# Threshold attention and ELU FFN on one core: the first sequence walked by query blocks instead of by pairs

## Chip, core and metric

The kernel runs on one core of a Trainium2 chip. The metric is the device time of one execution, in microseconds. Before the change it is 1313.69 us (median of 4 runs, 1313.1 to 1314.35).

## What is computed

Eight sequences (batch B = 8) of 576 tokens, 8 heads of 64 columns, all in fp32. Each query keeps only the keys whose score lies within tau of its best score; the attention output, 4608 tokens of 512 columns, goes through a feed-forward network (FFN) with an ELU between two matrices.

```python
scores = (q @ k.T) / 8
thresh = max(scores, axis=-1) - tau
scores = where(scores >= thresh, scores, -1e9)
attn = exp(scores - max(scores)); attn = attn / (sum(attn) + 1e-9)
x = (attn @ v)            # heads side by side: (4608, 512)
h = x @ w_in              # (4608, 2048)
g = where(h > 0, h, exp(min(h, 0)) - 1)
out = g @ w_out           # (4608, 512)
```

The weights come in as 64-bit floats, so they have to be turned into fp32 on the chip.

## The kernel before, in words

**Tiles.** Two heads make a pair; a sequence has NPAIR = 4 pairs, and there are 32 in all. The 576 queries of a pair are cut into four blocks of 128 for each head (i = 0 to 3, "two-head" steps) and the last 64 queries of both heads together (i = NC = 4, a "one-head" step): NB = 5 steps a pair. `steps` lists them as (pair, block).

**A step.** `scores` (L364) writes the scores of one block against all keys to PSUM, one tile for each head. `max_of` (L402, VectorE, here DVE) takes the negative maximum, `bound_of` (L406, GpSimd, here POOL) the threshold, `exp_of` (L416, ScalarE, here ACT) the exponential, `mask_of` (L425, DVE) multiplies it by the comparison with the threshold and sums the row. `reciprocal_of` (L431, L432) and `normalize` (L398, POOL) follow, in place in the tile w. Then w has to be transposed so that keys lie on partitions. There are two ways: `turn_parts` transposes 128x128 blocks on TensorE (PE, L435) into PSUM tiles rt and copies them on ACT (L451) to wTa or wTb; `turn_squares` (L509) transposes squares of 32x32 on DVE, writes them to DRAM ("there") and `fetch` reads them back in the right order. `values` (L570, L575) multiplies the transposed weights by v once a "part" is there: part 0 is blocks 0 and 1 (tile wTa), part 1 blocks 2, 3 and 4 (tile wTb, wider). `values_out` (L692, L698) copies the result to xt, the FFN's input.

**Fillers.** Where PE has little to do, `room` in `turn_parts` issues transposes of the identity into the same rt tile before the real ones, as many as were put in the list `spare`; `idle` does the same near the start.

**FFN.** The first sequence's 512 tokens (without the tails of 64) go through a plain FFN in two chunks of 256: `ffn1` (L733, with exp, minus one and ELU at L740, L743, L747) and `ffn2_plain` (L773). Each unit is cut in two halves; there are 64 halves. `needs` says how many of the 32 weight pieces must be converted before a unit may start. All later tokens use products with fewer multiplications (L1229, L1369), which need sums and differences of weight blocks: `make_in` (L852 to L854, DVE) writes three sums of each of eight units to DRAM ("win_sums"), `change_in` and `change_out` (POOL) change the weights in place.

**Weight pieces.** Each of the 32 pieces is loaded (`load_w`, 512 KB, tile wst, 4 buffers) and converted: `convert_rest` (L240, ACT), `convert_shift` (L246, DVE), `convert_add` (L252, POOL), `convert_abs` (L257, ACT), `convert_end` (L265, DVE).

**The order.** For the first 45 steps (MIDDLE = 45) `early_tasks` makes a list of tasks. Each has a due time: `begin` of its step plus an offset written in the code plus an offset from the table MOVED under a key such as "mask0b2" (task, head, stage letter, block). `do` runs tasks by due time, but any task that one needs runs first. The result is one fixed order of instructions for each engine and DMA queue; the due times themselves set no wait. The stages before the change:

- steps 0 to 19 (sequence 0, `per_seq` = 20): pair by pair; three score tiles in PSUM; fillers; no FFN;
- at step 20 `switch` closes the pool of three score tiles and opens two score tiles and two FFN banks;
- steps 20 to 34: the FFN halves by SHARES, two weight pieces a step;
- steps 35 to 44 (from SWITCH = 35): the tile pool "late" is there, every step is turned by `turn_squares`, the sums of `make_in` are made one unit a step, FFN halves by QUOTA (4, 4, 2, 3, 2).

SQUARES holds the steps turned on DVE: all from SWITCH on, and those of steps 22 to 34 whose MOVED entry "sq.." is over 1.0, which before the change is only step 33.

After step 44 another planner writes the wide part: scores of two blocks at a time (L622, L669 for the 64-query block), interleaved with the FFN of the sequence before. It runs from the first L669 at 289.8 us to the end.

Of the kernel before, what the change touches and what calls it, by code (L numbers as in the profile page):

```python
# [19 lines left out]
    "adda10": 2.75, "adda40": -0.7, "addb10": -0.45, "addb11": -0.96, "addb20": 0.4, "addb21": 0.54, "addb30": 0.08,  # L20
    "addb31": 0.42, "addb40": -0.13, "addb41": -0.45, "addz40": 1.52, "chd0": -1.67, "chd1": 0.66, "chd3": 5.2,
    "cka3": 1.4, "ckb3": -3.64, "ckc3": -0.46, "ckd3": -1.83, "ckz3": -1.37, "cqa2": 6.78, "cqb2": -3.01,
    "cqc2": -0.22, "cqd2": 2.27, "enda10": 2.38, "enda40": -0.2, "endb00": -0.03, "endb01": 1.48, "endb10": -0.28,
    "endb20": -1.25, "endb21": -1.07, "endb30": 1.25, "endb31": -0.02, "endb40": -0.99, "endb41": 0.29,
    "endz40": 1.58, "exp0a0": 0.24, "exp0a1": -1.03, "exp0a2": 0.05, "exp0a3": 1.07, "exp0a4": -0.35, "exp0b1": -0.97,
    "exp0b2": -0.37, "exp0b3": 1.51, "exp0b4": 0.45, "exp0c0": 0.41, "exp0c1": 3.53, "exp0c2": 0.65, "exp0c4": -0.53,
    "exp0d0": 0.12, "exp0d1": -2.91, "exp0d4": -0.42, "exp0z0": -1.78, "exp0z1": -0.69, "exp0z2": -1.71,
    "exp0z3": 1.1, "exp0z4": -1.32, "exp1a0": 0.27, "exp1a2": -1.45, "exp1b0": -0.12, "exp1b1": -0.6, "exp1b2": 0.26,
    "exp1b3": -0.56, "exp1c0": -1.22, "exp1c1": 1.42, "exp1c3": -0.54, "exp1d1": 0.28, "exp1d3": 0.23, "exp1z0": 4.71,
    "exp1z2": 0.39, "exp1z3": 2.23, "f0.0": -2.08, "f1.0": -0.13, "f1.1": 0.2, "f10.0": 0.05, "f11.0": -0.04,  # L30
    "f12.1": 0.12, "f13.1": -0.5, "f14.0": 0.02, "f15.1": -0.06, "f16.0": 0.04, "f16.1": 0.69, "f16.2": -0.14,
    "f17.0": -0.28, "f18.1": 0.12, "f2.0": -5.54, "f2.1": -0.25, "f2.2": 0.7, "f20.1": -1.03, "f21.0": 0.13,
    "f22.1": -0.19, "f23.0": 0.08, "f23.1": 2.72, "f23.2": 0.07, "f25.0": 0.39, "f26.0": -0.08, "f26.1": 0.42,
    "f3.0": 0.35, "f5.0": -0.32, "f5.1": 4.32, "f6.1": -0.54, "f7.0": -0.01, "f9.0": 0.35, "f9.1": 1.94,
    "fbound0": -0.14, "fbound1": 0.93, "fbound4": -0.36, "fe00": 0.1, "fe10": 0.37, "fe11": 0.3, "fe20": -0.6,
    "fetchc0": 0.68, "fetchc1": 1.8, "fetchc3": 1.11, "fetchc4": 2.68, "fetchd0": -1.89, "fetchd1": -3,
    "fetchd2": 0.42, "fexp00": 0.1, "fexp20": 0.25, "fexp31": 0.12, "ffetch0": 1.19, "ffetch1": -0.24,
    "ffetch2": -0.52, "ffetch3": -0.65, "fkcopy": -0.11, "floadk": -2.59, "floadq": 2.51, "fm00": -3.15,
    "fm01": -0.49, "fm11": -2.07, "fm20": 1.6, "fm21": -0.43, "fmask00": 1.48, "fmask01": -0.63, "fmask10": 0.68,
    "fmask11": 0.02, "fmask30": -0.16, "fmask31": 0.36, "fmask4": 0.2, "fmax00": -0.03, "fmax01": -0.65,  # L40
    "fmax10": 0.91, "fmax11": 0.5, "fmax20": -0.99, "fmax21": -0.15, "fmax30": 0.04, "fmax31": -0.17, "fmax4": 0.36,
    "fnorm01": 0.83, "fnorm10": -0.23, "fnorm11": -0.44, "fnorm20": 1.68, "fnorm31": -0.75, "fout1": 0.83,
    "fsum0": 0.21, "fsum2": 0.33, "fsum3": 0.21, "fturn0": 0.21, "fturn2": 0.46, "fturn3": -1.27, "fturn4": -3.36,
    "fx0": -0.43, "fx10": 3.03, "fx11": 2.86, "fx2": 1.4, "fx3": 0.53, "fx6": -1.72, "fx8": -0.33, "fx9": 1.95,
    "half0b0": 2.6, "half0b2": 0.03, "half0b4": -1.89, "half0c0": -0.35, "half0c1": 3.13, "half0c2": -1.05,
    "half0c3": 0.43, "half0c4": 0.59, "half0d0": 0.33, "half0d1": 2.22, "half0d2": 2.32, "half0d3": 1.9,
    "half0d4": -0.23, "half1b0": -0.69, "half1b2": 4.21, "half1b3": 2.24, "half1c0": -0.27, "half1c1": 1.44,
    "half1c3": -0.41, "half1d0": -1.15, "half1d1": -0.81, "half1d3": -1.93, "half2b0": 0.57, "half2b1": 3.37,
    "half2b2": 1.47, "half2b4": 4.56, "half3a4": -0.25, "half3b0": -0.69, "inc0": 0.26, "inc1": -0.32, "inc2": -0.84,
    "inc3": 0.62, "inc4": 1.01, "ind0": 3.59, "ind1": -0.55, "ind2": 0.71, "lka4": 0.31, "lkb4": -0.23, "lkc4": 2.75,  # L50
    "lkd4": -1.7, "lkz4": 1.33, "lqa3": -0.05, "lqb3": -0.78, "lqc3": 3.06, "lqd3": 1.57, "lqz3": 3.59, "lva3": -6.41,
    "lvb3": 0.23, "lvc3": -6.29, "lvd3": 0.25, "lwa40": -0.35, "lwb00": -0.29, "lwb01": 3.86, "lwb11": -1.49,
    "lwb20": 5.29, "lwb21": -0.43, "lwb30": 0.12, "lwb31": 0.49, "lwb41": -1.26, "lwz40": -0.42, "mask0a0": 1.44,
    "mask0a1": -0.72, "mask0a2": -1.16, "mask0a3": -0.52, "mask0a4": 0.63, "mask0b0": 2.64, "mask0b1": -0.06,
    "mask0b2": 4.79, "mask0b3": 0.64, "mask0b4": -0.11, "mask0c0": -1.59, "mask0c1": 3.33, "mask0c3": 0.31,
    "mask0c4": 0.37, "mask0d0": 3.54, "mask0d1": -0.89, "mask0d2": 0.28, "mask0d3": 1.22, "mask0z0": 1.27,
    "mask0z1": 2.9, "mask0z2": 0.32, "mask0z3": 1.31, "mask0z4": 0.56, "mask1a0": 1.27, "mask1a1": -0.16,
    "mask1a2": -4, "mask1a3": 1.13, "mask1b0": 3.3, "mask1b1": 1.74, "mask1b2": -0.32, "mask1b3": -0.38,
    "mask1c0": -1, "mask1c1": 2.6, "mask1c3": 0.06, "mask1d0": 3.74, "mask1d1": 0.12, "mask1d2": -0.2,
    "mask1d3": -0.98, "mask1z0": 0.69, "mask1z1": -1.47, "mask1z2": 0.5, "mask1z3": -4.11, "max0a0": -0.3,  # L60
    "max0a1": 1.72, "max0a2": 0.59, "max0a3": -0.46, "max0a4": 0.01, "max0b2": 1.44, "max0b3": 2.43, "max0b4": 0.13,
    "max0c0": 1.5, "max0c2": -3.36, "max0c3": -0.04, "max0c4": 1.16, "max0d0": 0.78, "max0d1": 2.46, "max0d2": -0.18,
    "max0d3": -0.86, "max0d4": 0.16, "max0z0": 2.5, "max0z1": -1.46, "max0z2": 6.32, "max0z3": -1.37, "max0z4": -0.85,
    "max1a0": 0.61, "max1a1": -0.07, "max1a2": -0.77, "max1a3": -0.22, "max1b0": 0.78, "max1b2": 0.03, "max1b3": 1.55,
    "max1c0": 0.62, "max1c1": -3.37, "max1c2": 1.27, "max1c3": -0.06, "max1d0": 0.68, "max1d1": -0.28, "max1d2": 3.35,
    "max1d3": 0.21, "max1z0": 2.29, "max1z1": 2.67, "max1z2": 9, "max1z3": 2.6, "norm0a0": 0.2, "norm0a1": -1.45,
    "norm0a2": -4.39, "norm0a3": -1.9, "norm0a4": -1.3, "norm0b1": -1.86, "norm0b4": -1.38, "norm0c0": 1.41,
    "norm0c1": -1.7, "norm0c3": 2.54, "norm0c4": 0.59, "norm0d0": 0.35, "norm0d1": 3.1, "norm0d2": -2.58,
    "norm0d3": -0.7, "norm0d4": -0.09, "norm0z0": -2.03, "norm0z1": -3.22, "norm0z2": -2.15, "norm0z3": -1.83,
    "norm0z4": -0.25, "norm1a0": -0.02, "norm1a1": -0.55, "norm1a2": 0.15, "norm1b0": 0.05, "norm1b1": 1.56,  # L70
    "norm1b2": -0.1, "norm1b3": -0.03, "norm1c0": -0.9, "norm1c1": 3.66, "norm1d0": -1.5, "norm1d1": -0.05,
    "norm1d2": -0.42, "norm1d3": -1.5, "norm1z0": 5.01, "norm1z1": -1.89, "norm1z2": -0.52, "norm1z3": -0.76,
    "outa4": -0.11, "outb1": -0.97, "outb4": -0.24, "outc1": 2.48, "outc4": -1.41, "outd1": -0.33, "outz1": 2.43,
    "outz4": -1.2, "part0a0": 0.88, "part0a1": 0.83, "part0a2": 0.68, "part0a3": -1.25, "part0b0": -0.58,
    "part0b1": -0.24, "part0b2": -0.82, "part0b3": -0.08, "part0b4": -1.67, "part0z2": -1.94, "part0z4": 0.79,
    "part1a1": -1.63, "part1a2": -1.63, "part1a3": -1.33, "part1a4": -2.94, "part1b0": 0.5, "part1b1": -1.16,
    "part1b2": 5.58, "part1b3": 1.91, "part1b4": -0.68, "part1z0": -4.29, "part1z1": -0.2, "part1z2": -0.4,
    "part1z3": 1.37, "part1z4": -1.08, "part2a0": -1.64, "part2a1": 3.26, "part2a2": 6.12, "part2a3": 1.34,
    "part2b0": 0.62, "part2b2": -0.41, "part2b3": 0.06, "part2z0": 2.23, "part2z1": 1.82, "part2z3": 0.07,
# [58 lines left out]
def kernel(  # L138
# [12 lines left out]
    P = 128  # L151
# [63 lines left out]
    for t in qds + vds:  # L215
        nc.gpsimd.memset(t, 0.0)
# [43 lines left out]
    def convert_end(i):  # L260

        progress[0] = i + 1
        if i in staged:
            sign, top = staged.pop(i)[:, :, 1].bitcast(I32), tops.pop(i).bitcast(FP32)
            nc.vector.scalar_tensor_tensor(pieces[i][1], top, 0.0, sign, ALU.max, ALU.mult)  # L265


    raws, pairs = {}, {}


    def load(pr, parts=("qm", "km", "v"), shared=False, queue=nc.sync):
# [649 lines left out]
    def early_tasks():  # L921
# [117 lines left out]
        for n in range(MIDDLE):  # L1039
# [8 lines left out]
            if n == per_seq:  # L1048
                task("switch", t, None, switch, *rooms)
# [591 lines left out]
```

## Time and profile before

The profiled execution took 1313.82 us and its span is 1312.0 us.

| what | before |
|---|---|
| PE busy (matmuls) | 1295.2 us, 99% |
| PEld busy (weight loads) | 1008.2 us, 77% |
| DVE busy | 1016.8 us, 77% |
| ACT busy | 559.5 us, 43% |
| POOL busy | 803.1 us, 61% |
| DMA, mean | 190 GB/s |
| first score, step 0 | 8.2 us |
| first score, step 10 | 53.4 us |
| first score, step 20 | 98.5 us |
| first score, step 35 | 208.2 us |
| first wide score (L669) | 289.8 us |

How to read it. A row "line engine op out<-in" names the line of the kernel, the engine and the tiles. PE is the matmul row and PEld the loads of its stationary operand, which overlap. In a table by windows, each engine's figure is its busy time in that stretch and (x..) its instructions. In a timeline, the first number is the start and the second the busy time of a group of like instructions; matmuls are pipelined, so the distance from one start to the next says what one costs the queue. An fp32 matmul of the program shows as two in the trace, a transpose as one. A bracket gives the idle time before the instruction and who ended it.

### The profile page before, as it was taken

To read this page: it belongs to the slowest core of one execution; us is meant where nothing else is said; L and a number is where in the kernel's file an instruction comes from. 1 tells how busy PE (TensorE), PEld (TensorE's weight loads), DVE (VectorE), ACT (ScalarE), POOL (GpSimd) and SP (SyncE) were. 2 spreads that over 40 slices of the span, in tenths; PEclk is the share of its full clock that TensorE was granted. 3 is DMA by queue.
4 is the path that set the end of the run, shared out by engine and by line. 5 is a ranking of instruction groups with operands and counts; after the bars stand their busy time and mean duration, and the time that the engine had idled before them with its cause. 6 is when DMAs were issued, how large, how long until landed. Compare 5 with 4: busy or idle time off the path is not lost.

```text
span 1312.0 us, 21958 instructions
## 1 busy us (share of the span) xinstructions
PE 1295.2 (99%) x6971; PEld 1008.2 (77%) x6971; DVE 1016.8 (77%) x2198; ACT 559.5 (43%) x1216; POOL 803.1 (61%) x1186
## 2 busy tenths in 40 slices
PE   9999999999999999999999999999999999999998
PEld 7667656546888787777778787777777888888887
DVE  5878886878888988898889979897989882545534
ACT  5767773225253535344444435352525260421320
POOL 4657874767567665766576747574858473624533
PEclk9999999999999999999999999999999999999999
DMA  6344655888888988898989888989899874221211
GB/s 137 77 103 123 165 126 140 239 231 214 231 232 237 266 224 250 216 264 212 245 216 257 236 226 234 252 239 240 233 253 252 219 220 171 92 73 61 92 61 32
DMA packets 323315, 248.94 MB, mean 190 GB/s; under 512 B 208768, under 2 KB 285056, under 8 KB 323200
## 3 DMA queue, kind: packets, MB, share of 16 engines
q1 hardware_dynamic: 320832, 247.25, 69.2%
q8 instruction: 55, 0.90, 0.3%
q10 hardware_dynamic: 2368, 0.30, 0.2%
q14 instruction: 60, 0.49, 0.1%
HBM read 162.40 MB, written 85.07 MB: 189 GB/s over the span
## 4 chain that ended last, share of the span: by engine, by line
PE 91%; DVE 4%; DMA 2%; POOL 1%; issue 1%; ACT 1%; SPq 1%; ACTq 0%; DVEq 0%; POOLq 0%
PE f L1369 29%; PE f L1229 28%; PE sc L622 8%; PE sc L682 7%; PE f L773 4%; PE rt L435 4%; PE sc L364 3%; PE f L733 3%; PE pv L575 2%; PE sc L674 1%; PE sc L669 1%; PE pv L570 1%; DVE w L425 1%; POOL w L398 0%; DMA vd<-in_v_dram 0%
## 5 line engine op out<-in xcount | busy, mean ns | idle before, releaser
L398 POOL TENSOR_SCALAR w<-w,rs 128x576 f32<-128x576 f32 x196 | 164.4, 846 | 81.8 <-DVE rs L432 64.7
L629 DVE TENSOR_REDUCE mx<-sc 128x1 f32<-128x576 f32 x207 | 148.3, 750 | 35.7 <-PE sc L622 33.0
L639 ACT ACTIVATE w<-sc,mx 128x576 f32<-128x576 f32 x115 | 83.0, 740 | 114.4 <-DVE mx L629 96.8
L1229 PE MATMUL f<-xt,sw 128*128 128x256 f32 x512 | 123.8, 384 | 0.9 <-ACT xt L692 0.5
L1229 PE MATMUL f<-xt,w_in_sb 128*128 128x256 f32 x512 | 122.4, 381 | 0.3 <-ACT w L1243 0.3
L635 POOL TENSOR_SCALAR th<-mx,ntau 128x2 f32<-128x2 f32 (+1 forms) x115 | 34.3, 298 | 141.7 <-DVE mx L629 141.7
L509 DVE STREAM_TRANSPOSE x<-w 128x512 f32<-128x512 f32 (+2 forms) x146 | 98.2, 706 | 13.3 <-POOL w L398 12.9
L1229 PEld LDWEIGHTS f<-xt,w_in_sb 128*128 128x128 f32 x512 | 96.1, 190 | 16.0 <-ACT w L1243 3.2
L1229 PEld LDWEIGHTS f<-xt,sw 128*128 128x128 f32 x512 | 93.7, 190 | 18.3 <-ACT xt L692 0.9
L622 PE MATMUL sc<-kT,qT 64*128 64x512 f32 (+4 forms) x736 | 107.5, 423 | 0.0
L1229 PE MATMUL f<-x,w_in_sb 128*128 128x256 f32 x448 | 106.1, 379 | 1.4 <-ACT g L1290 1.4
L1369 PE MATMUL f<-w_out_sb,g 128*128 128x256 f32 x448 | 107.1, 382 | 0.0
L622 PEld LDWEIGHTS sc<-kT,qT 64*128 64x128 f32 x736 | 80.8, 186 | 34.3 <-issue 16.8
L1369 PE MATMUL f<-w_out_sb,s 128*128 128x256 f32 x448 | 107.0, 382 | 0.0
L1369 PE MATMUL f<-t,s 128*128 128x256 f32 x448 | 105.8, 379 | 0.0
L1316 POOL TENSOR_TENSOR s<-g 128x256 f32<-128x256 f32 x104 | 80.5, 779 | 29.3 <-PE f L1369 20.1
L643 DVE SCALAR_TENSOR_TENSOR w<-sc,th,w 128x576 f32<-128x576 f32 x115 | 89.7, 810 | 10.7 <-ACT w L639 10.6
L1229 PEld LDWEIGHTS f<-x,w_in_sb 128*128 128x128 f32 x448 | 85.0, 190 | 13.3 <-ACT g L1290 1.8
L1369 PEld LDWEIGHTS f<-w_out_sb,g 128*128 128x128 f32 x448 | 84.1, 190 | 12.9 <-issue 0.7
L1369 PEld LDWEIGHTS f<-t,s 128*128 128x128 f32 x448 | 85.1, 190 | 11.6
L1369 PEld LDWEIGHTS f<-w_out_sb,s 128*128 128x128 f32 x448 | 84.2, 190 | 12.3
L398 POOL TENSOR_SCALAR e<-e,rs 128x576 f32<-128x576 f32 x92 | 68.4, 748 | 35.8 <-DVE rs L432 34.4
(188 smaller groups left out, 2855.9 us busy)
## 6 DMA issues: line engine op xcount, KB each, us to landing
there<-x SPq DMA_DIRECT2D x412, 144.0 KB, 3.5
wTb<-there SPq DMA_DIRECT2D x53, 576.0 KB, 6.5
wTa<-there SPq DMA_DIRECT2D x50, 576.0 KB, 4.7
sw<-win_sums SPq DMA_DIRECT2D x62, 384.0 KB, 4.4
t<-wout_sums SPq DMA_DIRECT2D x45, 512.0 KB, 5.6
qm<-in_q_dram SPq DMA_DIRECT2D x128, 72.0 KB, 4.8
vm<-in_v_dram SPq DMA_DIRECT2D x64, 128.0 KB, 3.2
wst<-in_moe_w_in_dram SPq DMA_DIRECT2D x16, 512.0 KB, 4.0
```

Source lines behind the costliest of these rows:

```text
L398: nc.gpsimd.tensor_scalar(wv, wv, st["rs"][:, h : h + 1], 1.0, ALU.mult, ALU.mult)
L435: nc.tensor.matmul(dst, src, ident, is_transpose=True, skip_group_check=True)
L509: nc.vector.transpose(x[:, :, c0 : c0 + nc_], src.rearrange("p (c g n) -> p g c n", c=nc_, n=T))
L622: on_banks(nc.tensor.matmul(o, qT[r, i * P : (i + 1) * P], kT[r, k0 : k0 + n], start=True, stop=True, skip_group_check=True), o)
L629: on_banks(nc.vector.tensor_reduce(st["mx"][:, h : h + 1], st["sc", h], axis=AX.XY if i == NC else AX.X, op=ALU.max, negate=True), st["sc" ...
L639: on_banks(nc.scalar.activation(st["e", h], st["sc", h], AF.Exp, bias=st["mx"][:, h : h + 1]), st["sc", h])
L643: on_banks(nc.vector.scalar_tensor_tensor(st["e", h], st["sc", h], st["th"][:, h : h + 1], st["e", h], ALU.is_ge, ALU.mult, accum_out=st[" ...
L682: on_banks(nc.tensor.matmul(o, vm[:, h, c], parts[part][:, g0:g1, h * (NC + 1) + c], start=False, stop=(c == NC - 1), skip_group_check=Tru ...
L773: nc.tensor.matmul(cur[c, i][:, :DM], hidden(c, ft % NU, 1)[:, 0, ft // NU, i], w_out_sb[:, ft], start=(ft == 0), stop=(ft == NFT - 1))
L1229: nc.tensor.matmul(loc["banks"][place], left[:, j], right[:, j], start=(begins and j == 0), stop=(j == 1), skip_group_check=True)
L1316: engine.tensor_tensor(o, x, y, op)
L1369: nc.tensor.matmul(place(m), lhs, rhs, start=(begins and v == 0), stop=(v == RU - 1), skip_group_check=True)
```

## The change

Sequence 0 is walked in two loops: first blocks 0 and 1 of all four pairs (steps 0 to 7), then blocks 2, 3 and 4 of all four pairs (steps 8 to 19). The inputs of the first FFN chunk, which are the tokens of blocks 0 and 1, are then there after step 9 instead of after step 17, and the FFN, the two-score-tile stage and the rate of two weight pieces a step begin at step LATE = 10 instead of 20.

- All q and k of the four pairs are prepared in steps 0 to 5 and live to step 19, so pairs 0 and 1 get tiles of their own (in the pool wstage, name "x", and zero-padded v tiles "vf").
- Part 0 of pairs 1 and 3 is collected in a wTb tile, so wTa and wTb alternate in the first loop.
- Fillers remain only in steps before 9.
- SHARES gives two halves a step for steps 10 to 34; QUOTA for the last ten steps falls to (2, 2, 2, 1, 2).
- `make_in` is cut into three tasks a unit. The sums of six units are made in steps 26 to 33, in buffers of the tile wst when the last weight piece is done; the last two units follow in steps 35 and 36.
- `reciprocal_of` is cut so that its sum (`total_of`) may stand earlier than its reciprocal.
- MOVED has 851 entries instead of 753; 172 keep their value. Seven steps (24, 25, 27, 28, 30, 31, 32) instead of one are turned on DVE before SWITCH.

The built program has 132 fillers instead of 230, 234 transposes of w on PE instead of 285, and on DVE 103 square transposes of 128x512 instead of 91. The number of scores, values, FFN halves and weight pieces is the same, and so is PE's order from the first wide score on.

```diff
-    for t in qds + vds:
+    vds_first = [wstage.tile([P, P], FP32, name=f"vf{i}", bufs=1) for i in range(NVD)]
+    for t in qds + vds_first + vds:
...
+        if pr < 2:
+            both = wstage.tile([P, 2 * S + TAIL], FP32, name="x", bufs=2)
+            qT, firsts[pr] = both[:, :S], both[:, S:]
+        else:
+            qT = qkp.tile([P, S], FP32, name="qT")
...
+            wide_one = part or pr < NPAIR and pr % 2
...
     steps = [(pr, i) for pr in range(NP) for i in ((0, 1, NC, 2, 3) if pr >= JOINED else range(NB))]
+    steps[:per_seq] = [(pr, i) for x in ((0, 1), (2, 3, NC)) for pr in range(NPAIR) for i in x]
+    LATE = 10
...
     def room_in(u):
+        if not late:
+            st = wstage.tile([P, WN, 2], U32, name="wst", bufs=4).rearrange("p n w -> p (n w)").bitcast(FP32)
+            return st[:, : 6 * P].rearrange("p (a k f) -> p a k f", a=3, k=2)
...
-    QUOTA = ((2, 2), (2, 2), (2, 0), (2, 1), (2, 0))
+    QUOTA = ((1, 1), (1, 1), (1, 1), (1, 0), (1, 1))
...
-        begin = [5.0 * min(n, per_seq) + 7.2 * max(0, n - per_seq) for n in range(MIDDLE + 4)]
-        kind = lambda n: "zabcd"[(n >= NB) + (n >= per_seq) + (n >= SWITCH) + (n >= SWITCH + NB)] + str(steps[n][1])
+        begin = [5.0 * min(n, LATE) + 7.2 * max(0, n - LATE) for n in range(MIDDLE + 4)]
+        kind = lambda n: "zaebcd"[(n >= 4) + (n >= LATE) + (n >= per_seq) + (n >= SWITCH) + (n >= SWITCH + NB)] + str(steps[n][1])
...
-        slots = [(n, x) for n in range(NB - 1, SWITCH)
-                 for x in range(steps[n][1] in (NB - 1, 1) if n < per_seq else 2)][: len(pieces)]
+        slots = [(n, x) for n in range(3, SWITCH) for x in range(n % 2 if n < LATE else 2)][: len(pieces)]
...
+        for u in range(NU):
+            n = 26 + 3 * u // 2 if u < NU - 2 else SWITCH + u - NU + 2
+            for x in range(3):
+                task(("in", u, x), begin[n] + 4.6 + 1.2 * x, f"in{x}{kind(n)}", lambda u=(u + 2) % NU, x=x: make_in(u, x),
+                     ("in", u, x - 1) if x else ("in", u - 1, 2) if u else None, "late" if u >= NU - 2 else ("end", len(pieces) - 1))
...
-                    if n < per_seq - 1 and x < 2 and not (n > 1 and steps[n + 1][1] in (2, NC)):
-                        spare.append((8 if x else 6) if n >= NB - 1 else (11 if x else 9))
+                    if n < LATE - 1 and x < 2 and not (n >= 2 and n % 2 == 0):
+                        spare.append((8 if x else 6) if n >= 4 else (11 if x else 9))
...
-    SHARES = ((1, 1, 1, 1), (0, 1, 1, 0), (1, 1, 1, 0), (0, 1, 1, 0), (1, 1, 1, 0))
+    SHARES = ((0, 0, 0, 0), (0, 0, 0, 0), (0, 1, 1, 0), (0, 1, 1, 0), (0, 1, 1, 0),
+              (0, 1, 1, 0), (0, 1, 1, 0), (0, 1, 1, 0), (0, 1, 1, 0), (0, 1, 1, 0))
```

## The prediction

> **What bounds the kernel now.** I first read the busy rows. PE is 99% busy over the whole span, so a stage gets shorter only where PE runs something that isn't needed, or waits. Then I cut the trace by windows at the score matmuls of steps 0, 10, 20 and 35 and at the first wide score (L669, 289.8 us).
>
> ```profile
> core 0: us, PE busy (x) PEld busy (x) DVE busy (x) ACT busy (x) POOL busy (x), PEclk, DMA share, GB/s
> 0.00:53.44 53.44, 50.32 (x350) 38.23 (x350) 36.82 (x91) 31.85 (x65) 25.90 (x60) 1.00 0.56 120
> 53.44:98.47 45.03, 44.27 (x314) 30.93 (x313) 36.11 (x87) 31.72 (x68) 27.24 (x49) 1.00 0.38 89
> 98.47:208.19 109.72, 107.74 (x535) 68.42 (x535) 87.89 (x180) 74.96 (x150) 80.30 (x100) 1.00 0.51 132
> 208.19:289.80 81.61, 79.06 (x335) 47.59 (x334) 66.73 (x144) 21.32 (x41) 57.75 (x82) 1.00 0.79 218
> 145.00:170.00 25.00, 24.19 (x124) 13.59 (x123) 23.88 (x47) 19.24 (x38) 22.45 (x27) 1.00 0.66 161
> ```
>
> PE is 94 to 98% busy in all of them at full clock (PEclk 1.00). VectorE (DVE) stands at 80 to 82% in steps 10 to 44. But PE's work before 98 us is partly filler: transposes of the identity whose result nobody reads. In steps 10 to 19 FFN matmuls take its place, so I see no reason for the clock to fall.
>
> ```profile
> L435 PE MATMUL rt<-ident,w 128*128 128x128 f32 x278 | 46.3, 281 | 3.2 <-POOL w L398 1.5 <-issue 1.0
> L435 PE MATMUL rt<-ident 128*128 128x128 f32 x230 | 32.1, 288 | 1.5 <-POOL ident masks.py:199 1.5
> ```
>
> All 230 fillers are issued before 98 us. What the filler hides is seen in the list of who waited for whom, for DVE before 98.47 us:
>
> ```profile
> DVE mx L402 <- PE sc L364: 6.9, 8, 1.5
> DVE w L425 <- ACT e L416: 6.8, 12, 0.9
> ```
>
> So the first 20 steps (4.5 us each) are set by the chain score, maximum, exponential, mask. Steps 20 to 44 (7.3 to 8.2 us) are set by PE, which does the FFN there. The PE timeline gives issue times, start to start:
>
> ```profile
> 93.62 1.14 PE L364 MATMUL sc<-kT,qd 128*128 128x288 f32 x4
> 94.59 0.27 PE L435 MATMUL rt<-ident,w 128*128 128x128 f32 x1
> ...
> 98.47 1.24 PE L364 MATMUL sc<-kT,qT 64*128 64x288 f32 x8
> 99.64 0.33 PE L435 MATMUL rt<-ident,w 128*128 128x128 f32 x1
> ...
> 101.27 7.07 PE L733 MATMUL f<-xt,w_in_sb 128*128 128x256 f32 x32
> 108.27 1.24 PE L364 MATMUL sc<-kT,qT 64*128 64x288 f32 x8
> 109.44 0.91 PE L570 MATMUL pv<-wTb,vd 128*128 128x384 f32 x2
> 110.28 2.37 PE L575 MATMUL pv<-wTb,vm 128*64 128x320 f32 x16
> ```
>
> Two-head scores take 1.17 us, one-head scores 0.97, four FFN halves 7.0 (1.73 to 1.75 each), values of a three-block part 3.15, of a two-block part 2.4 to 2.5, a transpose 0.11, a filler 0.115. For DVE, by the same reading: a maximum 0.67, a mask 0.74, sum and reciprocal 0.41, a weight shift 0.57 and its end 0.66, a q or k transpose 0.70, a square turned on DVE 1.42, a first-weight sum 0.54, an ELU 0.60.
>
> **What the change removes and adds, in the built order.** PE: fillers go from 230 to 132 (98 x 0.115 = 11.3 us) and transposes of w from 285 to 234 (51 x 0.11 = 5.6 us), because seven steps of sequence 1 instead of one are turned on DVE. FFN halves (64), scores and values keep their number. PE's need in the front part falls by some 17 us. DVE gets six squares more: 6 x 1.42 = 8.5 us. ScalarE loses the copies of those turns, about 1.4 us a step. Eighteen of the 24 weight sums move from steps 35 to 42 to steps 26 to 33, at the same price. SP gets six sets of four "there" writes and six fetches more; such writes land in 3.5 us and the fetches in 4.7 to 6.5, a step or more ahead of their values, so I cost them at nothing; without that lead each would hold the values by up to 10 us. After 289.8 us PE's order is the same in both kernels, so I leave the 1024.0 us from there to the profiled run's 1313.82 (span 1312.0 and 1.8 around it; the median, 1313.69, is 0.1 less).
>
> Counting the built order with these durations (DVE's sums meet the trace's busy time: 227 against 227.6 us):
>
> steps | before PE / DVE / measured | after PE / DVE
> 0-9 | 42.6 / 35.3 / 45.3 | 43.5 / 41.4
> 10-19 | 42.8 / 38.4 / 45.0 | 65.1 / 58.1
> 20-34 | 105.7 / 84.7 / 109.7 | 93.1 / 82.3
> 35-44 | 77.1 / 68.7 / 81.6 | 48.6 / 54.2
>
> PE's total falls, but DVE's rises and its slack goes: in steps 10 to 44 it needs 194.6 us beside PE's 206.8.
>
> **The step's loop.** With two score tiles, one step's scores wait for the masks of the step before. The DVE and PE timelines around step 35 show its links:
>
> ```profile
> 209.50 1.42 DVE L402 TENSOR_REDUCE mx<-sc 128x1 f32<-128x576 f32 x2 [1.39 <-PE sc L364]
> ...
> 212.40 0.82 DVE L425 SCALAR_TENSOR_TENSOR w<-sc,th,e 128x576 f32<-128x576 f32 x1 [1.47 <-DMA there<-x]
> ...
> 213.14 0.81 DVE L425 SCALAR_TENSOR_TENSOR w<-sc,th,e 128x576 f32<-128x576 f32 x1
> ```
>
> and on PE, one row between the two masks:
>
> ```profile
> 213.62 1.69 PE L364 MATMUL sc<-kT,qT 64*128 64x288 f32 x8
> ```
>
> The second mask ends at 213.95 and the scores, begun between the masks, at 215.31: with the start of the maximum 1.45 us. Two maxima take 1.34, the exponential about 0.55 more (between the 1.47 seen here and 0.17 elsewhere), two masks 1.48: a least loop of 4.8 us. DVE work in a gap lengthens it where it is longer than the gap. Step 26 after: maxima 1.34, a square 1.42 in the second gap, masks 1.48, then 0.41 and three sums 1.62 in the first: 6.27 us, against PE's 1.17 + 2 x 1.73 = 4.63. Step 11: DVE 6.89, PE 8.59 (scores, two halves, six transposes, values 3.15). I took the larger of the two in each step. For steps 20 to 44 before this gives 189.1 us, and 191.3 were measured (x 1.012). For steps 10 to 44 after it gives 34.0 + 31.8 + 32.8 + 32.4 + 34.1 + 31.4 + 32.6 = 229.1, so 231.8.
>
> Steps 0 to 9 have three score tiles; there the formula gives 49.9 before where 45.3 were measured (x 0.907), and 51.2 after, so 46.4. The steps are longer because no one-head step is among them and three pairs more are prepared. q of pair 1 is now turned in step 0, at about 10.9 us, on DVE with the first mask queued behind. Its last DMA is issued at 9.0 and lands in 2.5, so at 11.5. k of pair 2 comes behind 2 MB of weights, wanted at about 24. For these waits I add 1.5 us (0 if the loads are in time, 4 if both stall fully). At the end, step 44 has 4 us of DVE work after its last mask that the wide scores needn't wait for; PE no longer has halves there: -2.6.
>
> Sum: 8.2 (first score) + 46.4 + 1.5 + 231.8 - 2.6 = 285.3 against 289.8, -4.5. By five-step groups instead of steps (larger sum of each group, 220.3, x 1.047 as before: 182.8 to 191.3) it is 284.1, -5.7. I take -5: **1308.7 us**.
>
> A rule against this change: PE row first, weight loads fill 185 of 289.8 us (64%, 38.23 + 30.93 + 68.42 + 47.59). The Trainium skill, Perfetto Trace Analysis, Identifying the Most-Contended Engine, says matmul busy time overstates how near TensorE is to its limit and to judge it by the share of weight loads; by that DVE (78.5%) is the most contended engine, and the change, with 8.5 us more on it, would give about +8. The start-to-start times of the halves, with no gap between scores and halves, speak for PE being full after 98 us.
>
> **Rivals.**
> (a) PE stays the only bound; DVE's work fits into the gaps across steps. The window 145 to 170 speaks for it: DVE 95.5% and PE 97% busy together for 25 us. Then steps 10 to 44 take 206.8 x 1.047 = 216.5 and the front part 8.2 + 46.4 + 1.5 + 216.5 = 272.6: -17, 1297.
> (b) DVE becomes the bound and doesn't pack more tightly than now. In steps 20 to 44 it is at 80.2% by my sums; 82% over steps 10 to 44 means 194.6 / 0.82 = 237.3, 80.2% means 242.6: front part 293.4 to 298.7, so +3.6 to +8.9, about 1320. The place is steps 25 to 44, where squares stand in the DVE queue between maxima and masks and wait for POOL's normalizing. It decides from 83.3%: 194.6 over the 233.7 us that are left of 289.8 after 56.1. For it: its waits for scores and for POOL and ACT stay when PE's filler goes. Against: over steps 20 to 44 PE was late, so DVE was not pressed.
> (c) It does nothing: PE saves its filler, and DVE's work handed to the wide part's start, with the POOL sums, gives it back there: within 0.2% (2.6 us, about what a measurement of this kernel can tell).
>
> **Numbers.** Forecast 1304 to 1311 with 0.46, (a) 0.20, (b) 0.20, (c) 0.14. Faster by over 0.2%, below 1311.1: 0.66. Within: 0.14. Slower, over 1316.3: 0.20. Half of (a) and half of (b) are left out: the range is 1297 to 1319. The forecast's own range is 1303 to 1311.
>
> **What would show it.** The wide part's first score near 285 us; step 10's score at 56 (later shows the early loads); steps 10 to 19 at 6.8 us with PE over 95%; steps 35 to 44 at 6.4 with PE near 77% and DVE at 83 to 88%. PE over 95% up to 285 would show (a) half right; maxima waiting for scores and masks waiting for ACT by more than 25 us in steps 20 to 44 would show (b). I am wrong altogether if the part from the first wide score on is not 1024 us, or if values wait for the fetched squares.

## The result, and the profile after

No gain came out: 1314.83 us, the median of 42 runs (1309.18 to 1321.35), against 1313.04 us for the kernel before (60 runs, 1312.4 to 1315.05). The ratio is 1.0013, interval 1.0008 to 1.0017. The runs of the kernel before lie within 2.7 us, those of the kernel after are spread over 12.2 us. The profiled execution took 1312.49 us, 2.3 less than the median; its span is 1310.7 us, and the stages below are of this one execution. Of all executions on record one, of run 7 below (1866.11 us at a mean clock of 0.66), was slow throughout and is left out.

The stages, cut at the scores of steps 0, 10, 20, 35 and at the first wide score (now L701):

steps | before | forecast | after
---|---|---|---
start of step 0 | 8.18 | 8.2 | 7.93
0 to 9 | 45.3 | 47.9 | 53.75
10 to 19 | 45.0 | | 66.2
20 to 34 | 109.7 | | 98.5
35 to 44 | 81.6 | | 61.65
10 to 44 | 236.4 | 229.2 | 226.3
first wide score | 289.8 | 285.3 | 288.0
from there to the end of the span | 1022.2 | unchanged | 1022.7

The forecast of 47.9 holds its 1.5 us for early loads, that of 229.2 its 2.6 us at the tail. Steps 10 to 44 were to gain 7.2 us and gained 10.0; the first ten steps gave 8.5 of it back, 2.6 of them foreseen. The windows of the kernel after:

```profile
core 0: us, PE busy (x) PEld busy (x) DVE busy (x) ACT busy (x) POOL busy (x), PEclk, DMA share, GB/s
0.00:61.68 61.68, 54.58 (x366) 40.62 (x366) 42.95 (x102) 34.72 (x66) 29.57 (x64) 0.94 0.62 128
61.68:127.85 66.17, 65.14 (x345) 45.90 (x344) 57.87 (x113) 52.36 (x110) 59.24 (x71) 1.00 0.48 156
127.85:226.35 98.50, 95.67 (x469) 61.02 (x468) 80.76 (x187) 46.83 (x97) 51.34 (x84) 1.00 0.67 177
226.35:288.00 61.65, 54.43 (x207) 25.05 (x206) 49.79 (x115) 16.72 (x32) 48.26 (x73) 0.97 0.82 221
```

The column to look at is PEclk, ahead of the last two. It read 1.00 in every stage before; now it is 0.94 in the first and 0.97 in the last. Finer windows of the same kernel, without the header:

```profile
20.00:25.00 5.00, 5.00 (x41) 3.58 (x41) 3.92 (x9) 3.52 (x8) 3.01 (x7) 1.00 1.08 349
25.00:30.00 5.00, 2.81 (x16) 1.47 (x12) 1.90 (x5) 1.82 (x4) 0.85 (x2) 0.88 0.72 109
30.00:35.00 5.00, 5.00 (x20) 3.94 (x20) 3.72 (x9) 1.48 (x3) 2.68 (x5) 0.50 0.76 135
35.00:40.00 5.00, 4.87 (x36) 3.59 (x36) 3.31 (x9) 3.13 (x6) 1.32 (x3) 0.94 0.15 31
```

From 25 to 30 us PE works for only 2.81 us; then, at a clock of 0.50, it seems fully busy but gets 20 instructions done, not 41 as from 20 to 25 us. (A busy share says nothing here; the count does.) What stands behind the idle time is a chain over three queues. The SP queue of the kernel after:

```profile
13.78 2.16 SPq L297 DMA_DIRECT2D qm<-in_q_dram  x4
15.98 1.92 SPq L249 DMA_DIRECT2D wst<-in_moe_w_in_dram  x4
18.00 5.70 SPq L297 DMA_DIRECT2D km<-in_k_dram  x4
```

Its DVE, with the wait in the bracket, and its PE:

```profile
28.10 0.78 DVE L330 STREAM_TRANSPOSE kT<-km 128x576 f32<-128x576 f32 x1 [3.56 <-DMA km<-in_k_dram]
28.80 0.38 DVE L262 TENSOR_SCALAR wtop<-wst 128x512 uint32<-128x512 uint32 x1
29.11 0.81 DVE L445 SCALAR_TENSOR_TENSOR w<-sc,th,e 128x576 f32<-128x576 f32 x1
```

```profile
25.52 1.22 PE L462 MATMUL rt<-ident,w 128*128 128x128 f32 x8
28.93 3.39 PE L384 MATMUL sc<-kT,qT 64*128 64x288 f32 x8 [2.19 <-DVE kT L330]
32.26 0.47 PE L462 MATMUL rt<-ident,w 128*128 128x128 f32 x1
32.52 2.13 PE L462 MATMUL rt<-ident 128*128 128x128 f32 x9
```

k of pair 2 is issued behind four weight pieces (2 MB), and its four issues alone take SP 5.70 us where the other sets of four up to 41 us take 2.1 to 2.4. It lands at 28.0. DVE waits 3.56 us with both masks of step 3 behind it. PE waits 2.19 us and then runs the scores of step 4 in 3.39 us, where run 6 below, at full clock, needs 2.34 (0.39 of it a wait for a mask), and nine fillers in 2.13 instead of 1.15.

There are three more idle stretches of PE of about 2 us, all in the last stage. In the kernel before, from the first scores to the wide part, none was longer than 0.82 us.

```profile
237.98 1.94 PE L384 MATMUL sc<-kT,qT 64*128 64x288 f32 x8 [1.95 <-DVE w L445]
...
252.42 1.21 PE L384 MATMUL sc<-kT,qd 128*128 128x288 f32 x4 [2.64 <-DVE w L445]
...
283.95 0.67 PE L602 MATMUL pv<-wTa,vd 128*128 128x256 f32 x2 [2.20 <-issue]
284.55 3.50 PE L607 MATMUL pv<-wTa,vm 128*64 128x256 f32 x16
```

The first two end when DVE's masks end. The third ends at 283.95 us with no releaser that the profile names; the fetch of squares to wTa that these values need was issued at 278.81, and such fetches land after 5.1 to 5.6 us, so 283.9 to 284.4. In the kernel before, two FFN halves, 3.60 us together, stood there:

```profile
281.33 3.60 PE L773 MATMUL f<-w_out_sb,g 128*128 128x512 f32 x8
284.76 0.59 PE L570 MATMUL pv<-wTa,vd 128*128 128x256 f32 x2
```

After the third the clock is 0.50 again (values in 3.50 instead of 1.95 us); after the first two it stayed at 1.00 in this execution. The mean granted clock differs from run to run, 0.991 to 0.998, and the lower it is, the longer the time (correlation -0.80 over the 42 runs; the fitted line has 1309.8 us at full clock and 9.9 us more for each 0.01). The kernel before shows about 0.999.

### The profile page after: what moved, and what is told of

It reads as the page before. It is cut to its first block, busy times and chain, and to the rows that moved or that the text cites. A ratio compares the mean times of both kernels' runs of the same rounds, so it can differ in the third digit from the quotient of the medians.

```text
span 1310.7 us, 21723 instructions
## 1 busy us (share of the span) xinstructions
PE 1284.1 (98%) x6822; PEld 995.7 (76%) x6822; DVE 1022.5 (78%) x2217; ACT 550.0 (42%) x1196; POOL 799.8 (61%) x1188
## 4 chain that ended last, share of the span: by engine, by line
PE 86%; DVE 4%; DMA 3%; POOL 2%; issue 2%; ACT 2%; SPq 1%; DVEq 0%; POOLq 0%; ACTq 0%
PE f L1424 29%; PE f L1284 28%; PE sc L654 8%; PE sc L714 7%; PE sc L384 3%; PE f L765 2%; PE f L805 2%; PE pv L607 2%; PE rt L462 2%; DVE w L445 1%; PE sc L706 1%; PE sc L701 1%; ACT e L436 1%; DVE mx L422 1%; POOL w L418 1%
## 5 line engine op out<-in xcount | busy, mean ns | idle before, releaser
L541 DVE STREAM_TRANSPOSE x<-w 128x512 f32<-128x512 f32 (+2 forms) x163 | 107.2, 692 | 13.7 <-POOL w L418 13.5
L654 PE MATMUL sc<-kT,qT 64*128 64x512 f32 (+5 forms) x736 | 108.0, 423 | 0.0
```

The costliest lines, as they stand in the source:

```text
L541: nc.vector.transpose(x[:, :, c0 : c0 + nc_], src.rearrange("p (c g n) -> p g c n", c=nc_, n=T))
L654: on_banks(nc.tensor.matmul(o, qT[r, i * P : (i + 1) * P], kT[r, k0 : k0 + n], start=True, stop=True, skip_group_check=True), o)
```

## The experiments

**Theory.** The change gains what it should in steps 10 to 44; the gain goes into the granted clock, which the idle stretches of PE let fall. **Rivals.** The loss is the wait for k itself; or DVE, with its additional squares and sums, bounds steps 20 to 44; or the fillers that remain stand on the path of steps 0 to 9. Each run was compared with runs of the kernel before on the same chip.

**1. k of pair 2 ahead of the weights.** In the task "lw" the first pieces get a later due time:

```diff
-(begin[m] + 8.0 if i > 3 else 4.8)
+(begin[m] + 8.0 if i > 3 else 8.9)
```

> Edit of the changed kernel: the first four weight pieces (2 MB) are issued on SP behind the k of pair 2 instead of ahead of it; the order on all other engines is the same. Theory A (early loads): in the changed kernel k of pair 2 lands at 28.0 us, DVE waits 3.6 us for it with two masks queued behind, PE idles 2.2 us and the granted clock falls to 0.50 in 30 to 35 us; together this is about 6 to 7 of the 8.4 us by which steps 0 to 9 got longer. Then step 10 begins near 56 us instead of 61.7, the clock in 25 to 40 us is 1.00, and the time is 1308 to 1309. Rival B (the steps themselves): ten two-head steps with more preparation need these 53.7 us anyhow, loads or not; then step 10 stays at 60 to 62 us and the time at 1313 to 1315. Rival C: the weights come too late instead, ACT waits for the first piece, and the time stays or rises.

Measured: 1313.03 us, ratio 0.9995 (0.9984 to 1.0005). The wait for k is gone, the clock is 1.00 from 20 to 60 us, step 10 comes at 57.97 and step 35 at 222.65, both 3.7 us earlier; for step 10 that lies between the theory's 56 and rival B's 60 to 62. But the span is 1311.5 us, no shorter. In the windows of this run the lead shrinks at the wait of step 37, which is as long as before (1.95 us) and this time costs the clock:

```profile
230.00:235.00 5.00, 3.04 (x8) 1.08 (x7) 4.96 (x12) 1.41 (x2) 5.00 (x7) 1.00 0.67 176
235.00:240.00 5.00, 4.99 (x12) 2.35 (x12) 3.31 (x8) 0.84 (x2) 4.92 (x6) 0.66 0.64 222
```

```profile
234.27 2.15 PE L384 MATMUL sc<-kT,qT 64*128 64x288 f32 x8 [1.95 <-DVE w L445]
236.35 3.42 PE L805 MATMUL f<-w_out_sb,g 128*128 128x512 f32 x4
```

An FFN half takes 3.42 instead of 1.98 us, and step 38 leads by 2.1 us instead of 3.7. Another 1.4 us goes where a wide FFN matmul waits for win_sums to be read back; the rest was not traced. So the wait for k is part of the loss and not the whole of it.

**2. The first idle stretch filled.** In `scores`, ahead of step 4:

```diff
+        if (pr, i) == (2, 0):
+            for _ in range(20):
+                transpose(scs[0][:, 0, :P], ident)
```

> Edit of the changed kernel: 20 transposes of the identity (20 x 0.115 = 2.3 us at full clock) ahead of the scores of step 4, where PE waits for k of pair 2; the loads stay as they are. It separates the wait from the clock. Theory A says both count: DVE still waits 3.6 us, but PE is kept busy, step 4's scores take 1.24 us instead of 3.39 and the transposes behind them 1.2 instead of 2.1: step 10 at 58 to 59 us and the time 1311 to 1312.5. If the clock's fall cost nothing beside the wait, step 10 stays at 61 to 62 us; if the clock falls in spite of it, likewise.

Measured: 1313.12 us, ratio 0.9995 (0.9985 to 1.0005). k is as late as before (DVE waits 3.4 us), but the clock stays at 1.00 behind step 4's wait and step 10 comes at 59.63, 2.1 us earlier. This execution had a fall of its own near the start, from 8.55 to 11.97 us; run 6, with the same filler and no fall, has step 10 at 59.18, 2.5 earlier. So of the 3.7 us of run 1, 2 to 2.5 are the clock. This lead, too, gets smaller at step 37 (step 38 at 246.45 against 246.63), where the clock is at half from 237.25 to 240.66.

**3. Without the seven squares ahead of step 35.**

```diff
-SQUARES = [*range(SWITCH, MIDDLE), *(n for n in ... if MOVED.get(f"sq{n}", 0.0) > 1.0)]
+SQUARES = [*range(SWITCH, MIDDLE)]
```

> Edit of the changed kernel: none of the steps 20 to 34 is turned on DVE; the seven are turned on PE and copied by ACT (the due times are not made anew). PE gets 7 x 9 transposes, about 7 us, DVE loses 7 x 1.42 = 10 us. Theory A (PE binds steps 10 to 34, DVE's loop is just under it): steps 20 to 34 get 3 to 7 us longer, time 1317 to 1322. Rival D (the six squares added on DVE are what made the change fail): steps 20 to 34 get shorter by 3 to 6 us, time 1309 to 1312.

Measured: 1323.64 us, ratio 1.0067 (1.0055 to 1.0079). Steps 20 to 34 take 107.05 us (129.33 to 236.38) instead of 98.5. Turning seven steps on DVE is worth 8.5 us there, more than the 3 to 7 expected, and rival D is out. PE's busy time rises by 6.0 us (95.67 to 101.69) and its idle time by 2.5, while DVE's falls by 9.5: PE, not DVE, was short. The 2.5 us of idle time were not taken apart; ACT got the copies, and the due times are those of the other order.

**4. The six units' weight sums on POOL instead of DVE.**

```diff
-        nc.vector.tensor_tensor(sw[:, x], a, b, ALU.add)
+        (nc.vector if late else nc.gpsimd).tensor_tensor(sw[:, x], a, b, ALU.add)
```

> Edit of the changed kernel: the 18 first-weight sums of steps 26 to 33 are made on POOL (0.75 us each) instead of DVE (0.54 each), in the same order. It takes 9.7 us from DVE where it needs 56.9 us of about 66 and puts 13.5 on POOL. Theory A: steps 25 to 34 alternate between PE and DVE as the bound, so 2 to 5 us are won, time 1310 to 1313. If PE alone binds there: within 1 us of 1314.8. If POOL's thresholds and normalizing behind the sums become late: 1316 to 1320.

Measured: 1313.73 us, ratio 1.0006 (0.9993 to 1.0018). Step 20 comes at 128.38, step 35 at 226.36: 98.0 against 98.5 us, not the 2 to 5 that theory A hoped for. PE is busy for 95.49 of these 98.0 us (95.67 of 98.5 before the edit). The sums cost next to nothing on DVE, since PE fills these steps.

**5. Three FFN halves from steps 20 to 34 into 35 to 44.** In SHARES, the first block's row of steps 20 to 34:

```diff
-              (0, 1, 1, 0), (0, 1, 1, 0), (0, 1, 1, 0), (0, 1, 1, 0), (0, 1, 1, 0))
+              (0, 1, 0, 0), (0, 1, 1, 0), (0, 1, 1, 0), (0, 1, 1, 0), (0, 1, 1, 0))
```

> One FFN half less in each two-head first-block step of the stage of steps 20 to 34; the three halves are done in steps 35 to 44, behind the others. Theory (steps 20 to 34 are bound by PE, steps 35 to 44 by the loop of scores, DVE's maxima and masks, in which PE idles): step 35's score comes about 5 us earlier than the 226.35 us of the kernel after (3 halves of 1.73 us), the stage 35 to 44 stays within 2 us of 61.65 because the halves fall into PE's idle time, and the first wide score comes 3 to 5 us earlier; time 1309 to 1312. Rival (DVE's loop bounds steps 20 to 34 as well): step 35 comes at the same time, and the time is that of the kernel after or longer by up to 5 us.

Measured: 1321.54 us, ratio 1.0069 (1.0049 to 1.0090). Neither side had it: with 5.2 us less of PE work, steps 20 to 34 take 101.2 us (126.61 to 227.85), 2.7 more. The PE timeline of this run, from step 25:

```profile
161.68 1.24 PE L384 MATMUL sc<-kT,qT 64*128 64x288 f32 x8
162.85 1.98 PE L805 MATMUL f<-w_out_sb,g 128*128 128x512 f32 x4
165.63 1.94 PE L384 MATMUL sc<-kT,qT 64*128 64x288 f32 x8 [0.80 <-DVE w L445]
...
188.23 1.97 PE L765 MATMUL f<-xt,w_in_sb 128*128 128x256 f32 x8 [2.07 <-DVE g L779]
```

Step 25 loses a half of 1.73 us and gets shorter by 1.05 (3.95 against 5.00), because the masks are late at once by 0.80 us; at this step DVE's loop lies just under PE's. At 188 us a half of another FFN unit stands where its room is still held by an ELU (g L779). That the halves could move freely was wrong; the queue of units and the ELUs move with them. Steps 35 to 44 take 64.67 us, 3.0 more (the first wide score is at 292.52), where at most 2 were expected. So this run says how near the two bounds are, not which of them holds in general.

**6. All four idle stretches filled.** Run 2's filler, and matmuls of kT with itself that nobody reads, four ahead of step 37's scores, five ahead of step 39's, four ahead of the last values of part 0:

```diff
+    WARM = {(NPAIR + 3, 2): 4, (NPAIR + 3, NC): 5}
...
+                for _ in range(WARM[pr, i]):
+                    nc.tensor.matmul(rt[:, : 2 * P], kT[:, TAIL : TAIL + P], kT[:, TAIL : TAIL + 2 * P], start=True, stop=True)
...
+        if (pr, part) == (2 * NPAIR, 0):
+            for _ in range(4):
+                nc.tensor.matmul(pv[:, : 2 * P], kT[:, TAIL : TAIL + P], kT[:, TAIL : TAIL + 2 * P], start=True, stop=True,
...
```

> The kernel after, with matmuls whose result nobody reads put into the four idle stretches of PE of 2 to 2.6 us: 20 identity transposes ahead of step 4's scores (as in the run that filled that gap alone), four matmuls of 128x256 ahead of step 37's scores, five ahead of step 39's, four ahead of the last values of part 0. No load, wait or order of another engine changes. Theory (each idle stretch of about 2 us can drop the granted clock to half for some microseconds, and how often that happens in a run makes the run's time): mean granted clock at least 0.998 in nearly all runs, against 0.995 for the kernel after, spread of the runs below 4 us against 12 us, and a median of 1309 to 1311. Rival (the spread of the runs has another cause, the clock only goes along with it): median and spread as with the one gap filled, 1313 us and 6 us.

Measured: 1311.14 us (11 runs, 1309.45 to 1313.23), ratio 0.9981 (0.9973 to 0.9990). The mean clock is 0.998 to 1.000 in all runs and the spread 3.8 us. Work that does nothing makes the kernel faster, by 0.3% against the kernel after (0.9981 against 1.0013). The windows of this run, by five microseconds where the clock had fallen and by stages:

```profile
25.00:30.00 5.00, 4.79 (x38) 3.50 (x34) 1.71 (x3) 1.94 (x4) 0.69 (x3) 1.00 0.50 94
30.00:35.00 5.00, 4.74 (x38) 4.14 (x40) 4.47 (x12) 2.85 (x6) 3.39 (x6) 1.00 0.76 125
...
0.00:59.18 59.18, 54.63 (x385) 41.40 (x386) 42.69 (x102) 34.63 (x66) 29.57 (x64) 1.00 0.65 133
59.18:125.42 66.24, 65.15 (x346) 45.90 (x344) 58.04 (x113) 51.86 (x109) 59.25 (x71) 1.00 0.48 156
125.42:223.59 98.17, 96.02 (x469) 60.93 (x468) 80.65 (x187) 47.16 (x97) 51.30 (x84) 1.00 0.65 175
223.59:284.58 60.99, 58.57 (x231) 29.37 (x230) 49.18 (x113) 17.09 (x33) 47.63 (x72) 1.00 0.85 227
```

From 30 to 35 us PE now gets 38 instructions done instead of 20. The first wide score comes at 284.58. The fills of the last stage take no time, since they end before the wait does:

```profile
233.10 1.89 PE L1017 MATMUL rt<-kT 128*128 128x256 f32 x8
235.22 1.94 PE L387 MATMUL sc<-kT,qT 64*128 64x288 f32 x8 [0.23 <-DVE w L448]
...
278.83 1.89 PE L607 MATMUL pv<-kT 128*128 128x256 f32 x8
281.44 0.70 PE L610 MATMUL pv<-wTa,vd 128*128 128x256 f32 x2 [0.72 <-DMA wTa<-there]
```

Behind the last fill the profile does name the fetched squares (wTa<-there) as what the values wait for.

**7. Run 1's load and the fills**, those of run 6 without the one ahead of step 4, which waits no more, and another ahead of the first values:

```diff
+        if (pr, part) == (0, 0):
+            for _ in range(10):
+                transpose(pv[:, :P], ident)
```

> The k load of pair 2 issued ahead of the first weight pieces (as in the run that did that alone, where PE's first idle stretch was gone and its second lead was lost again behind 222 us), and PE's other idle stretches filled: ten identity transposes ahead of the first values, and the three later fills of the run that fills all. Theory (clock): the 3.7 us gained by step 35 are no longer lost at half clock in steps 37 and 38; mean clock at least 0.998, median 1306 to 1309.5. Rival (the lead is lost to waits of DVE and of the weight sums' loads, not to the clock): 1311 to 1313, as with the load alone.

Measured: 1310.22 us (7 runs), a little above the theory's 1306 to 1309.5 and below the rival's 1311; ratio 0.9977 (0.9966 to 0.9987). Step 35 comes at 223.55, in run 6 at 223.59: with the clock held, the earlier load adds nothing that can be measured. This and run 10 are the fastest versions, 0.23% under the kernel before.

**8. The kernel before without the fillers of steps 0 to 18.**

```diff
-                        spare.append((8 if x else 6) if n >= NB - 1 else (11 if x else 9))
+                        pass
```

> The kernel before without the fillers that stand ahead of the real transposes in steps 0 to 18 (the 44 near the start stay). Theory (fillers keep the granted clock up): PE idles by 1 to 2 us in each of these steps, the granted clock is below 0.9 in the first 98 us, and the time is longer by 3 to 20 us. Rival (fillers only pass the time): steps 0 to 19 take their 4.5 us each, set by the chain score, maximum, exponential, mask, clock 1.00, and the time is that of the kernel before within 1 us.

Measured: 1319.51 us, ratio 1.0041 (1.0029 to 1.0054), mean clock 0.991 to 0.996. The same effect without anything of the change. PE's idle stretches are short here: none between the first scores and 98 us is longer than 1.54 us, and those just ahead of the four falls are at most 1.14 us. So the clock can fall without a stretch of 2 us. This run's windows, and those of the kernel before:

```profile
60.00:65.00 5.00, 3.75 (x17) 2.53 (x17) 4.14 (x10) 3.29 (x6) 3.90 (x6) 0.63 0.16 61
65.00:70.00 5.00, 5.00 (x22) 1.91 (x20) 3.41 (x9) 1.41 (x3) 2.20 (x5) 0.69 0.00 0
```

```profile
60.00:65.00 5.00, 5.00 (x38) 3.18 (x36) 4.25 (x10) 3.23 (x7) 3.90 (x7) 1.00 0.00 1
65.00:70.00 5.00, 4.75 (x37) 3.27 (x34) 3.84 (x9) 3.34 (x9) 2.44 (x5) 1.00 0.24 64
```

**9 and 10. Run 7 with half, and with none, of the 88 fillers of steps 0 to 8.** The line of run 10 has `pass` in place of the second:

```diff
-                        spare.append((8 if x else 6) if n >= 4 else (11 if x else 9))
+                        spare.append((4 if x else 3) if n >= 4 else (5 if x else 4))
```

> The kernel with the k load ahead and all idle stretches filled, with the fillers ahead of the transposes of steps 0 to 8 cut to about half (88 to 42 or so). Theory P (with the k wait gone, the fillers themselves stand on the path of steps 0 to 9): these 46 fillers of 0.115 us give up to 5 us: step 10's score near 54 to 56 us instead of 58.65, clock still 1.00, time 1306 to 1308. Rival C (chain of score, maximum, exponential, mask and normalizing sets these steps): step 10's score stays within 1 us of 58.65 and the time within 1 us of 1310.3; the clock may fall.

> The same kernel with none of the 88 fillers ahead of the transposes of steps 0 to 8. Theory P: step 10's score 6 to 10 us earlier, if the clock holds; with the clock lost, as the kernel before lost it without its fillers, steps 0 to 9 get back what they gain, mean clock 0.992 to 0.997, runs spread over more than 4 us, median above that of the run with half the fillers. Rival C: step 10's score no earlier than 58 us and time 1311 to 1317 with a fallen clock.

Measured: 1310.88 us, ratio 0.9981 (0.9973 to 0.9990), and 1310.18 us, ratio 0.9977 (0.9968 to 0.9986). Step 10 comes at 60.21 and 58.79, against 58.65. Without its fillers the stage is no shorter: they are not on the path. That the chain of the step sets steps 0 to 9 follows from this by elimination. In these two profiles the clock falls once each, in run 9 from 25.37 to 28.78 us, and there it costs 1.6 us: PE works again at 24.64 us behind its wait, in run 7 at 24.67, but step 4 comes at 30.96 against 29.37, and step 10 is as late. In run 10 it falls here:

```profile
15.00:20.00 5.00, 4.92 (x21) 3.42 (x21) 4.03 (x10) 3.37 (x8) 2.92 (x7) 0.66 0.79 127
```

Run 10's fall cost nothing that shows (step 10 at 58.79). A fall costs only as far as PE has no slack behind it: run 8, whose four falls make 20.5 us at half clock and so take up to 10.2 us of PE's work, lost 6.4 us.

## Why the prediction was wrong

The step that failed is "so I see no reason for the clock to fall". It was argued from the mean PE share, and a mean can't show single idle stretches of 1 to 2 us. The prediction named two of the places itself: the load of k of pair 2 behind 2 MB of weights, and a last stage with "PE near 77%" behind DVE's loop. It priced the first as a wait only (1.5 us, 4 at most) and the second not at all. And "I cost them at nothing", of the fetched squares, failed once: the last values of part 0 waited 2.2 us for theirs, since the FFN halves that had covered it were gone by the new QUOTA; the forecast counted their going as a gain of 2.6 us. That values would wait for fetched squares was one of the prediction's own signs of being wrong. Filling the four stretches, with every wait left as it is, moved the ratio from 1.0013 to 0.9981, about 4 us of the 6.1 us that lie between the forecast of 1308.7 and the median of 1314.83. The other 2 us were not traced. (The prediction gives the forecast's own range once as 1304 to 1311 and once as 1303 to 1311.)

At full clock its sum was near: 285.3 us for the first wide score, 284.58 in run 6, whose profiled execution took 1309.67 us. But two terms were off there and cancel.

- Steps 0 to 9: 46.4 + 1.5 forecast, 51.15 in run 6 (49.9 in run 1, without the wait for k). The factor 0.907, taken from the stage before the change with its pairs in sequence, doesn't hold for the new order; without it the formula had 51.2. Runs 9 and 10 show that the fillers don't set this stage; which link of the chain makes it longer than before was not taken apart.
- Steps 10 to 44: 229.2 forecast, 226.3 measured, 225.4 in run 6. Steps 10 to 19 came at 6.62 us with PE at 98% (6.8 and over 95% forecast), steps 35 to 44 at 6.17 (6.4) with DVE at 81% (83 to 88%) and PE at 88% (77%). Taking the larger of the two engines' sums in each step fits these times; run 5 shows both bounds within 1 us of each other at step 25.

Rival (a), PE alone as bound with 216.5 us, is out: these steps took 9.8 us more, and DVE's masks hold PE up ahead of steps 37 and 39 by 4.6 us together. Rival (b), DVE as bound at 82% or less, is out: 226.3 us is less than its 237.3, and maxima waiting for scores (11.8 us) and masks waiting for ACT (3.4) add up to 15 us after step 20, not to more than 25. Rival (c) has the time right for the wrong reason: nothing was given back in the wide part, which took 1022.7 against 1022.2 us. The rule on weight loads, weighed in the prediction with DVE as the most contended engine and about +8 (the page calls matmul busy time no good measure and names the share of peak arithmetic (MFU) beside the weight loads; that it overstates, at 99%, is the prediction's reading), is not borne out in steps 10 to 44: they gained, and run 3 shows that work moved from PE to DVE paid.

## What to carry to other kernels

Read the PE timeline of a new order for idle stretches from about 1 us on, alone or several within some 3.4 us, and not only for the share. Price one as the wait and, where PE has no slack behind it, up to half of the time at half clock besides (1.7 us of 3.4). Where such a wait can't be removed, matmuls that nobody reads and that end before it does are free and hold the clock. When runs of a kernel spread more than they did, compare their mean granted clocks before looking for a cause in the queues.

## What the runs showed of the hardware

Idle time of PE of 1 to 2.7 us could halve the clock: 0.88, 0.50 and 0.94 in the five-microsecond windows from 25 us on come to 6.8 us at half clock; 0.66 in run 1's window comes to 3.4, and 0.63 and 0.69 in run 8 to 6.8 again. So it lasted 3.4 us or twice that. Within one execution the falls begin whole multiples of 3.41 us apart: at 28.78 and 284.78 us in the kernel after (75 times), at 16.93, 37.41, 61.30 and 85.20 in run 8 (6, 7 and 7 times). It looks as if the clock were set anew at the marks of a fixed grid. Windows cut at these marks, the first two of the kernel after, the third of run 1, the last of run 8:

```profile
233.58:236.99 3.41, 2.45 (x6) 0.76 (x4) 3.41 (x8) 1.41 (x2) 3.41 (x4) 1.00 0.47 105
236.99:240.40 3.41, 2.41 (x10) 1.31 (x11) 2.66 (x8) 0.04 (x1) 3.41 (x6) 1.00 1.03 338
232.46:235.88 3.42, 1.59 (x8) 1.00 (x8) 2.80 (x10) 0.27 (x1) 3.42 (x6) 1.00 1.00 306
81.78:85.20 3.42, 2.29 (x12) 1.11 (x10) 3.35 (x10) 3.02 (x8) 0.89 (x2) 1.00 0.26 68
```

The same wait of 1.95 us at step 37 cost the clock in run 1 and not in the kernel after: there a mark cuts it into 0.96 and 0.99 us, in run 1 it lies nearly whole in one window (1.82 us idle), and the clock is at half from 235.88 us on. In run 8 one stretch of 1.13 us was enough, and the clock is at half from 85.20. In the twelve profiles, up to 300 us, no such window at full clock with less than 1.0 us of idle PE had a fall behind it and every one with more than 1.92 us had; between, both occur (1.04 us in run 8 with a fall, 1.91 us in run 9 without). So idle time alone doesn't decide it, and what else does was not found. Where the grid lies differs from profile to profile, and 42 executions of the kernel after got mean clocks from 0.991 to 0.998.

The Trainium skill, TensorE: Matmul & The Clock Gate, Part 1: The HAM clock gate, tells of a monitor with a window of 3.4 us that runs freely, and of half clock after an idle window. The lengths of 3.4 and 6.8 us, the grid and the luck of the phase agree with it; but no window ahead of a fall in full clock was idle throughout here, 2.67 of 3.41 us being the most. Its section HAM oscillation — how this bites in real kernels puts the rule as no idle gaps over about 3.4 us; here stretches of 1.13 us (run 8) to 2.66 us (run 3) were followed by half clock, and the measurement decides.

The issue of four loads took SP 5.70 us behind four loads of 512 KB, and 2.1 to 2.4 us for the other such sets up to 41 us; the next, at 41.52 us, took 4.10.
